# Weights for dx turned in the first attention chunk and loaded plainly later, with dW2 blocks fetched three ahead

## Chip, cores, metric

One core of one Trainium2 chip. The metric is the device time of one execution in microseconds (us), of which the median over several executions is quoted; the profile shows one execution. "Turned" means transposed by the DMA on its way.

## The reference

A transformer block with adaptive layer norm, forward and all its gradients (S = 2048, D = 512, 32 heads of 16, MLP width F = 1792, bfloat16), cut to what matters:

```python
mod = (silu(c) @ w_mod).reshape(c.shape[0], 6, 1, -1)
sa, ca, ga, sb, cb, gb = (mod[:, 0], ..., mod[:, 5])
h = layernorm(x) * (1 + ca) + sa
x = x + ga * attention(h, A_wqkv, A_wo)
h = layernorm(x) * (1 + cb) + sb
x = x + gb * (relu(h @ B_w1 + B_b1) ** 2 @ B_w2 + B_b2)
...
out, vjp = jax.vjp(f, A_x, A_wqkv, A_wo, B_w1, B_b1, B_w2, B_b2, c, w_mod)
grads = vjp(grad_out)
```

Two gradients matter here. The gradient of `A_x` goes through the layer norm and needs `A_wqkv`, its rows scaled by 1 + ca and then transposed; the kernel calls this WmT, and uses it at the very end. The gradient of `B_w2` (dW2) is a product of the MLP's activations (kept in DRAM as `aT_d`) with the gradient at the MLP's output.

## The kernel before

The kernel runs the forward attention in four chunks of queries, then a middle phase (last MLP chunk, gradients dW1 and dW2 of the MLP), then the backward attention. Background generators feed TensorE (PE) with work: `fill.take(n)` in the middle phase emits n of their steps. The middle phase prepared WmT itself:

```python
        fill.until("half")                       # dW2 is half done
        ws = self.load_wmt(self.open_pool("wkt", bufs=1))
        self.T0, pieces = self.load_group(0)     # first group of the backward
        pieces = self.pair_pieces(0, 0) + pieces
        for n, (d, sr) in enumerate(pieces):
            nc.sync.dma_start(d, sr)
            fill.take(7)
            if n % 3 == 2 and ws:
                self.turn_wmt(*ws.pop(0))
        for w in ws:
            self.turn_wmt(*w)
        fill.drain()
    ...
    def load_wmt(self, sb):
        self.WmT = self.wp.tile([P, 3 * DT, D], BF16, name="WmT")
        ws = []
        for kt in range(DT):                     # DT = 4
            w = sb.tile([P, 3 * D], BF16, name="w_kt", bufs=DT)
            nc.sync.dma_start(w[:], io["A_wqkv"][kt * P:(kt + 1) * P, :])
            nc.scalar.activation(w[:], w[:], ACT.Copy, scale=self.opcaT[:, kt:kt + 1])
            ws.append((kt, w))
        return ws

    def turn_wmt(self, kt, w):
        self.nc.sync.dma_start_transpose(self.WmT[:, :, kt * P:(kt + 1) * P], w[:])
```

dW2 takes one turned block of activations for 16 matmuls, and fetches two blocks ahead:

```python
        def load(ft):
            r = sb.tile([P, ST, P], BF16, name="a_blk", bufs=3)
            nc.sync.dma_start_transpose(r[:], self.aT_d[ft])
            ...
        load(0); load(1)
        yield 0
        for ft in range(FT):                     # FT = 14
            if ft + 2 < FT:
                load(ft + 2)
            a, w2_blk = blks[ft]
            pt = self.dps.tile([P, 512], F32, name="dps")
            for st in range(ST):                 # ST = 16
                nc.tensor.matmul(pt[:], lhsT=a[:, st, :], rhs=g_tm[:, st, :], ...)
                yield 1
```

During the first attention chunk a generator projects q, k and v for the later heads (groups g); ScalarE (ACT) is the bound there, with one exp after the other (busy for 66.9 of 67 us from 135 to 202 us in the kernel before):

```python
        for g in range(1, NQ):
            ...
            yield (-g, 0)
            if g == 2:
                yield from self.gen_mod()
            elif 3 <= g < 3 + self.SC:
                yield from self.gen_vt(4 * (g - 3))
            for s0 in range(512, S, 512):
                yield from self.gen_fm(self.mps, 0, g - 1, s0)
```

The softmax here doesn't subtract the row's maximum and nothing guards it: scores larger than these inputs give would overflow.

## Time and profile before

| | before |
|---|---|
| time, median of 3 runs | 2691.65 us (2686.25 to 2698.53) |
| span of the profiled execution | 2680.6 us |
| PE busy | 93% |
| ACT busy | 86% |
| dW2, first to last matmul | 67.2 us |

### The profile page before, as it was taken

How to read it: one execution, taken by the hardware profiler on the slowest of the kernel's cores; microseconds unless marked ns; L12 is line 12 of the kernel's file. 1: busy time of each engine (PE TensorE's matmuls, PEld its weight loads, DVE VectorE, ACT ScalarE, POOL GpSimd, SP SyncE). 2: the span in 40 equal slices, each digit the busy share in tenths (PEclk: the TensorE clock that was granted, in tenths of full speed). 3: DMA queues.
4: the chain of work that ended last, by engine and by line, in shares of the span. 5: the costliest groups of instructions: out<-in, count | busy, mean ns of one | idle time of the engine just before them, and what ended most of it. 6: DMA issues, size and time to landing. Idle time of an engine off the chain costs nothing.

```text
span 2680.6 us, 76637 instructions
## 1 busy us (share of the span) xinstructions
PE 2486.6 (93%) x30980; PEld 1229.1 (46%) x31210; DVE 1764.2 (66%) x3650; ACT 2307.9 (86%) x3728; POOL 393.4 (15%) x661
## 2 busy tenths in 40 slices
PE   5999999999999998898999999999999999999997
PEld 2555555555555554653443444444444434443443
DVE  4222222423423344656999999999999999999857
ACT  4999999999999995326999999999999999999823
POOL 2234531320221131351000000000000000000032
PEclk9999999999999999999999999999999999999999
DMA  4367752440441244999999999999999999999997
GB/s 146 91 146 160 175 121 69 114 110 21 124 115 54 86 98 122 222 224 173 201 196 198 199 196 198 200 202 202 194 199 200 203 198 200 196 197 209 208 217 175
DMA packets 1198027, 439.59 MB, mean 164 GB/s; under 512 B 1135430, under 2 KB 1159496, under 8 KB 1197672
## 3 DMA queue, kind: packets, MB, share of 16 engines
q1 hardware_dynamic: 1165608, 342.70, 70.4%
q0 software_dynamic: 29952, 89.36, 11.5%
q8 instruction: 244, 4.00, 0.6%
q10 hardware_dynamic: 2112, 2.62, 0.3%
q14 instruction: 111, 0.91, 0.1%
HBM read 83.30 MB, written 67.11 MB: 56 GB/s over the span
## 4 chain that ended last, share of the span: by engine, by line
PE 29%; DMA 24%; issue 3%; ACT 2%; DVE 1%; POOL 0%; SPq 0%; POOLq 0%; ACTq 0%; DVEq 0%
DMA dsT<-ds 22%; PE st L1315 11%; PE acckv L1217 6%; PE accq L1239 5%; ACT pu L1319 1%; PE dps L848 1%; PE g3ps L1421 1%; PE dp L1260 1%; DMA a_blk<-aT_d 1%; PE dxhps L1396 1%; PE st L1279 1%; PE dps L797 1%; PE st L1228 1%; DMA wo<-in_A_wo_dram 0%; PE g3ps L1408 0%
## 5 line engine op out<-in xcount | busy, mean ns | idle before, releaser
L1262 DVE TENSOR_TENSOR ds<-dp,pu 128x512 bf16<-128x512 f32 x2048 | 1243.0, 679 | 62.5 <-PE dp L1260 53.9
L1319 ACT ACTIVATE pu<-st 128x512 bf16<-128x512 f32 x2048 | 1082.8, 613 | 104.7 <-PE dp L1260 67.5
L348 ACT ACTIVATE pu<-st 128x1024 bf16<-128x1024 f32 x1024 | 943.0, 1072 | 6.7 <-PE st L345 4.7
L345 PE MATMUL st<-QTm,KTq 128*128 128x512 bf16 x1923 | 579.4, 377 | 31.1 <-ACT pu L348 9.6
L309 PEld LDWEIGHTS <-pu 128*128 128x128 bf16 x8192 | 347.4, 96 | 235.4 <-ACT pu L348 0.4
L1239 PEld LDWEIGHTS <-dsT 128*128 128x128 bf16 x8192 | 244.9, 96 | 273.7 <-issue 205.3
L309 PE MATMUL accbank<-Vaug,pu 128*128 128x17 bf16 x8192 | 357.7, 171 | 7.1 <-ACT pu L348 0.3
L1260 PE MATMUL dp<-m,dOTq 64*128 64x512 bf16 x1024 | 339.5, 383 | 0.0
L1260 PE MATMUL dp<-m,q 64*128 64x512 bf16 x1024 | 338.7, 384 | 0.7 <-DVE g2w L854 0.7
L1315 PE MATMUL st<-m,q 64*128 64x512 bf16 x1024 | 321.3, 383 | 8.4 <-ACT pu L1319 6.5
L1315 PE MATMUL st<-m,QTq 64*128 64x512 bf16 x1024 | 320.6, 383 | 6.3 <-ACT pu L1319 4.5
L345 PEld LDWEIGHTS <-KTq 128*128 128x128 bf16 x2048 | 194.1, 96 | 187.0 <-issue 132.6
L1370 POOL DMA_DIRECT2D O_tm<-O_d x2 | 1.8, 912 | 1323.1 <-PE accq L1239 1323.0
L1239 PE MATMUL accq<-q,dsT 128*128 128x16 bf16 x4096 | 150.8, 170 | 31.4 <-DMA dsT<-ds 31.3
L1239 PE MATMUL accq<-Kg,dsT 128*128 128x16 bf16 x4096 | 148.8, 170 | 28.9 <-DMA dsT<-ds 28.4
L1217 PE MATMUL acckv<-ds,Qg 128*16 128x512 bf16 x1024 | 155.3, 383 | 0.3 <-DVE ds L1262 0.2
L1217 PE MATMUL acckv<-pu,q 128*16 128x512 bf16 x1024 | 155.3, 383 | 0.0
L1217 PE MATMUL acckv<-ds,q 128*16 128x512 bf16 x1024 | 155.3, 384 | 0.0
L1217 PE MATMUL acckv<-pu,dOg 128*16 128x512 bf16 x1024 | 154.9, 383 | 0.0
L1280 ACT COPY dsT<-st 128x512 bf16<-128x512 bf16 x256 | 152.5, 596 | 1.5 <-PE st L1279 1.4
L316 DVE RECIPROCAL rl<-accbank 128x4 f32<-128x4 f32 x128 | 22.9, 179 | 163.2 <-PE accbank L309 163.2
L1315 PEld LDWEIGHTS <-q 64*128 64x128 bf16 x1024 | 58.1, 94 | 123.1 <-issue 104.2
(313 smaller groups left out, 2627.7 us busy)
## 6 DMA issues: line engine op xcount, KB each, us to landing
KTq<-KTq_d POOLq DMA_DIRECT2D x24, 512.0 KB, 3.6
duT_d<-auT POOLq DMA_DIRECT2D x4, 1792.0 KB, 8.8
aT_d<-rT POOLq DMA_DIRECT2D x4, 1792.0 KB, 13.7
KTq_d<-KTq SPq DMA_DIRECT2D x32, 128.0 KB, 1.8
QTq_d<-ev_fm SPq DMA_DIRECT2D x32, 128.0 KB, 2.0
VTq_d<-vT POOLq DMA_DIRECT2D x4, 1024.0 KB, 6.2
O_d<-O POOLq DMA_DIRECT2D x4, 1024.0 KB, 5.4
m<-KTq_d SPq DMA_DIRECT2D x32, 128.0 KB, 3.6
```

The lines of the kernel that those rows point to most:

```text
L309: nc.tensor.matmul(acc[:, a, sub, :], lhsT=pu[:, a, sub * P:(sub + 1) * P], rhs=Vaug[:, kb, h, :], start=(kb == 0 and a == 0 and sub == 0) ...
L345: nc.tensor.matmul(stt[:, a, :], lhsT=KT[:, kb * P:(kb + 1) * P], rhs=QTm[2 * jp + a][:], start=True, stop=True)
L348: nc.scalar.activation(pu[:], stt[:], ACT.Exp, scale=self.scale)
L797: nc.tensor.matmul(g4[:, kt, :], lhsT=xh2[:, st, kt * P:(kt + 1) * P], rhs=du[:, st, :], start=(st == 0), stop=(st == ST - 1))
L848: nc.tensor.matmul(pt[:], lhsT=a[:, st, :], rhs=g_tm[:, st, :], start=(st == 0), stop=(st == ST - 1))
L1217: nc.tensor.matmul(acckv[r:r + DH, :], lhsT=T[n][:, ib, col:col + DH], rhs=src[:, a, :], start=(ib == 0), stop=(ib == ST - 1))
L1239: nc.tensor.matmul(accq[:, ib, a, :], lhsT=dsT[:, (i * 2 + a) * 4 + sub, :], rhs=T["K"][:, 4 * c + sub, col:col + DH], start=(c == 0 and i ...
L1260: nc.tensor.matmul(dp[:], lhsT=T["dOT"][rd, ib * P:(ib + 1) * P], rhs=masked["VT"][2 * jp + a][rd, 512 * c:512 * (c + 1)], start=True, sto ...
L1262: nc.vector.tensor_tensor(dsg[:, i, a], dp[:], pu[:, a, :], ALU.mult)
L1280: nc.scalar.copy(dsT[:, 0:4, :], tp[:])
L1315: nc.tensor.matmul(stt[:], lhsT=T["QT"][rs, q], rhs=masked["KT"][2 * jp + a][rs, c0:c0 + 512], start=True, stop=True)
L1319: nc.scalar.activation(pu[:, a, :], stt[:], ACT.Exp, scale=self.scale)
```

## The change

The intent is to empty the DMA queue in front of dW2's last blocks. The weights are in SBUF during the first attention chunk anyway; so they are scaled on GpSimd, turned, and stored to a DRAM scratch `WmT_d` there, in four rounds. In the middle phase three plain loads of WmT, behind everything else, take the place of four loads, four scalings and four turns. Besides, dW2 gets a fourth block buffer and fetches three ahead, and the background work between the pieces is `take(8)` each time.

```diff
+        self.WmT_d = self.dram("WmT_d", [P, 3 * DT, D], BF16)
 ...first chunk's generator
             yield (-g, 0)
+            if 2 < g < 3 + self.DT:
+                w = self.qkv_eb.tile([P, 3 * self.D], BF16, name="wm_s", bufs=1)
+                nc.gpsimd.tensor_scalar(w[:], self.wq[:, g - 3, :], self.opcaT[:, g - 3:g - 2], 1.0, ALU.mult, ALU.mult)
 ...
             for s0 in range(512, S, 512):
                 yield from self.gen_fm(self.mps, 0, g - 1, s0)
+            if 2 < g < 3 + self.DT:
+                wt = self.qkv_eb.tile([P, 3 * self.DT, P], BF16, name="wm_t", bufs=1)
+                nc.sync.dma_start_transpose(wt[:], w[:])
+                with nc.allow_non_contiguous_dma(reason="256B runs"):
+                    nc.gpsimd.dma_start(self.WmT_d[:, :, (g - 3) * P:(g - 2) * P], wt[:])
 ...middle phase
-        ws = self.load_wmt(self.open_pool("wkt", bufs=1))
         self.T0, pieces = self.load_group(0)
-        pieces = self.pair_pieces(0, 0) + pieces
-        for n, (d, sr) in enumerate(pieces):
+        pieces = self.pair_pieces(0, 0) + pieces + self.load_wmt()
+        for (d, sr) in pieces:
             nc.sync.dma_start(d, sr)
-            fill.take(7)
-            if n % 3 == 2 and ws:
-                self.turn_wmt(*ws.pop(0))
-        for w in ws:
-            self.turn_wmt(*w)
+            fill.take(8)
 ...dW2
-            r = sb.tile([P, ST, P], BF16, name="a_blk", bufs=3)
+            r = sb.tile([P, ST, P], BF16, name="a_blk", bufs=4)
 ...
+        load(2)
         for ft in range(FT):
-            if ft + 2 < FT:
-                load(ft + 2)
+            if ft + 3 < FT:
+                load(ft + 3)
 ...load_wmt, its body now
+        return [(self.WmT[:, n:n + DT, :], self.WmT_d[:, n:n + DT, :]) for n in range(0, 3 * DT, DT)]
```

More of the change, by code (lines that the diff above doesn't have):

```diff
@@ L388, in gen_open @@
         xm1T = self.xm1T = sb.tile([P, DT, S], BF16, name="xm1T")
-        wq = sb.tile([P, DT, 3 * D], BF16, name="wqkv")
+        wq = self.wq = sb.tile([P, DT, 3 * D], BF16, name="wqkv")
         wpads = self.wpads = [sb.tile([P, DT, NQ, P], BF16, name=f"wpad{t}") for t in range(2)]
@@ L745, in last_chunk @@
         fill.until("half")
-        ws = self.load_wmt(self.open_pool("wkt", bufs=1))
         self.T0, pieces = self.load_group(0)
-        pieces = self.pair_pieces(0, 0) + pieces
-        for n, (d, sr) in enumerate(pieces):
+        pieces = self.pair_pieces(0, 0) + pieces + self.load_wmt()
+        for (d, sr) in pieces:
             nc.sync.dma_start(d, sr)
-            fill.take(7)
-            if n % 3 == 2 and ws:
-                self.turn_wmt(*ws.pop(0))
-        for w in ws:
-            self.turn_wmt(*w)
+            fill.take(8)
         fill.drain()
-        for name in ("wkt", "dw2", "dw1", "e0", "dwps", "tps", "mps2", "mps"):
+        for name in ("dw2", "dw1", "e0", "dwps", "tps", "mps2", "mps"):
             self.close_pool(name)
@@ L1141, in open_bwd, with load_wmt @@
         self.qp = self.open_pool("p5q", bufs=1, side="right")
-    def load_wmt(self, sb):
-        nc, io = self.nc, self.io
+    def load_wmt(self):
         D, DT = self.D, self.DT
         self.WmT = self.wp.tile([P, 3 * DT, D], BF16, name="WmT")
-        ws = []
-        for kt in range(DT):
-            w = sb.tile([P, 3 * D], BF16, name="w_kt", bufs=DT)
-            nc.sync.dma_start(w[:], io["A_wqkv"][kt * P:(kt + 1) * P, :])
-            nc.scalar.activation(w[:], w[:], ACT.Copy, scale=self.opcaT[:, kt:kt + 1])
-            ws.append((kt, w))
-        return ws
-    def turn_wmt(self, kt, w):
-        self.nc.sync.dma_start_transpose(self.WmT[:, :, kt * P:(kt + 1) * P], w[:])
+        return [(self.WmT[:, n:n + DT, :], self.WmT_d[:, n:n + DT, :]) for n in range(0, 3 * DT, DT)]
     def load_group(self, g):
```

## The prediction

> **What bounds the kernel now.** I read the page first, for the stages. The span is 2680.6 us in 40 slices of 67 us.
>
> ```profile
> PE   5999999999999998898999999999999999999997
> ACT  4999999999999995326999999999999999999823
> DMA  4367752440441244999999999999999999999997
> PE 29%; DMA 24%; issue 3%; ACT 2%; DVE 1%; POOL 0%; SPq 0%; POOLq 0%; ACTq 0%; DVEq 0%
> ```
>
> Slices 1 to 15 (to about 1005 us) are the forward attention, with PE and ACT both at 9; slices 19 to 38 are the backward attention, with PE, ACT and DMA at 9; in between lies a middle phase (last MLP chunk, dW1, dW2, loads for the backward) in which ACT falls to 2. The last line is the chain that ended last; it names PE and DMA, and by line mostly the turning of ds in the backward attention, which the change does not touch. So the change can only act in two places: the first attention chunk, where it adds work, and the end of the middle phase, where it takes work out.
>
> Then the chain in order of time, around the end of the middle phase:
>
> ```profile
> 1158.82 0.22 PE dps L848
> ...
> 1186.80 3.40 PE dps L860 x16
> 1190.21 10.11 DMA a_blk<-aT_d
> 1200.36 5.32 PE dps L848 x16
> ...
> 1208.05 9.47 DMA a_blk<-aT_d
> 1217.57 8.70 PE dps L848 x32
> ```
>
> dW2 is L848 (224 matmuls) plus 16 of L860 for db2. From the ninth block on, the chain runs through the turned loads of a_blk and no longer through PE. How long PE was really idle is in the timeline of PE (start, length, and in brackets the idle time before it and what ended it):
>
> ```profile
> 1158.66 17.43 PE L848 MATMUL dps<-g_tm,a_blk 128*128 128x512 bf16 x78
> ...
> 1200.36 5.31 PE L848 MATMUL dps<-g_tm,a_blk 128*128 128x512 bf16 x16 [3.20 <-DMA a_blk<-aT_d]
> 1207.00 3.63 PE L848 MATMUL dps<-g_tm,a_blk 128*128 128x512 bf16 x15 [1.33 <-DVE g2w L854]
> 1217.57 8.69 PE L848 MATMUL dps<-g_tm,a_blk 128*128 128x512 bf16 x32 [6.95 <-DMA a_blk<-aT_d]
> ```
>
> Undisturbed, 78 matmuls take 17.43 us, or 0.2235 us each. All 240 at that pace are 53.6 us. They took from 1158.66 to 1226.26, 67.6 us. The **excess is 14.0 us**: 11.66 us of idle time (3.20, 1.33, 6.95, and 0.18 in another line) and some 2.3 us because what runs after an idle stretch is slower (16 in 5.31 us is 0.33 us each; the mean granted clock from 1200 to 1220 us is 0.77 where it is 1.00 before).
>
> Why the blocks are late is in the DMA view of 1185 to 1226 us:
>
> ```profile
> DMA packets 19063, 9.86 MB, mean 240 GB/s; under 512 B 17108, under 2 KB 17108, under 8 KB 19060
> q1 hardware_dynamic: 18449, 8.25, 96.5%
> q0 software_dynamic: 611, 1.57, 15.4%
> w_kt<-in_A_wqkv_dram SPq DMA_DIRECT2D x4, 384.0 KB, 8.9
> a_blk<-aT_d SPq DMA_TRANSPOSE x5, 6.4
> WmT<-w_kt SPq DMA_TRANSPOSE x4, 5.3
> ```
>
> The sixteen engines are full: the sync queue alone is at 96.5% of their time. In the same view of 1158 to 1185 us that queue is at 72.4% with eight a_blk and nothing else, so one a_blk costs 0.724 x 27 / 8 = 2.44 us of all the engines, against the 16 x 0.2235 = 3.58 us in which PE uses it up. The block stream alone is carried; the stream plus w_kt, WmT and eleven pieces of the first group is not. In the queue's own timeline, issuing the a_blk of 1190 us takes 7.24 us where one takes 3 in the median.
>
> [...] here a_blk's 0.524 MB in 2.44 us is 215 GB/s[...]. [...] the new store writes runs of 256 B, and no row of the trace times exactly that. [...] the trace's row is 1753 ns for a 128x1792 tensor_scalar.
>
> **The change part by part.**
>
> Removed from the middle phase: four loads of w_kt (4 x 0.393 = 1.57 MB), four ACT scalings of 1.57 us (ACT is idle there anyway, so worth nothing), and four SBUF transposes (1.57 MB, by a_blk's cost 4 x 0.75 x 2.44 = 7.3 us of all engines). Added there: three plain loads of WmT, 1.57 MB. They are the last of the fourteen pieces, so in the queue they stand behind the last a_blk, and WmT is first read at 2575 us: nothing waits for them. What must land before dW2 ends falls from 9.8 MB to about 4 a_blk (2.1) + pieces (2.36) + w2 loads and dW2 stores (1.57) = 6.0 MB, an estimate from the sizes in that view. At its mean of 240 GB/s that is 25 us.
>
> The fourth buffer: the load of block ft+4 waits until block ft is done and is used four blocks later, so its lead grows from two blocks to three, 7.2 to 10.7 us. Landing takes 5.4 to 10.1 us (median 6.4) here, so three blocks cover even the worst seen. Also one more block is already under way when the pieces start. Block 6 ends at about 1158.7 + 7 x 3.58 = 1183.7 us; from then PE needs one more block and the 112 matmuls behind it, until 1158.7 + 53.6 = 1212.3 us, 28.6 us. The 25 us of transfers fit, with 3.6 us to spare. PE should bound dW2 again: I take back 12.5 of the 14.0 us and leave 1.5 for a stall or two.
>
> After dW2 the first exp of the backward waits for the last dW2 store (2 us from issue to landing now, with 31 us of idle ACT before). That stays, and the WmT loads are then still in flight (6.0 + 1.57 MB at 240 GB/s end 31.5 us after 1183.7, at 1215): I charge 1 us.
>
> Added in the first chunk, in four rounds between about 135 and 270 us: a POOL tensor_scalar of 128x1536, by the row above 1753 x 1536/1792 = 1.5 us; one SBUF transpose of 1.8 us of the engines; one POOL store with 1536 runs, which should cost POOL about 1 us to issue, as the 0.92 us of the 1024-run dOp_d store. That is 2.5 us on a POOL that is busy 13 to 15 of 34 us there, with the DMA engines at 0.6 to 0.76; ACT is full (34.0 of 34) and gets nothing added, and PE gets no instruction. So it lies beside the bound. What could reach it is POOL standing still until the turned tile lands (3 to 5 us), with the next q load behind it; those loads are issued more than half a unit of 17 us early. I charge 0.5 us in all.
>
> Sum: -12.5 + 1 + 0.5 = **-11 us**. 2691.65 - 11 = about 2681 us, 0.4% less.
>
> **The rivals.** (1) *The transfers still bound dW2's end*: the margin of 3.6 us is smaller than what a slow mix of transfers can take, and SP issues its last pieces without waiting, so WmT shares the engines with the store traffic. For it: [...]a transpose moves slower than a plain load. Against it: w_kt and WmT's transposes, over 30% of the bytes, are gone from in front. It would leave a gain of 5 us, 2687 us. (2) *POOL stalls the first chunk*: for it, POOL [...]already waits for turned tiles (41.3 us for ev_tm from KTq between 60 and 260 us); four stalls of 5 us reaching ACT would eat the gain, giving 2691 to 2701 us. Against it: the lead of the q loads. (3) *The backward starts earlier but is not shorter by as much*: its first group must have landed, and its 1330 us run by the turned ds at full DMA share, so a start with a backlog can shift its pattern by some us either way: 2676 to 2688 us. (4) *The full 14 us and a little of the clock*: 2677 us.
>
> **Range and chances.** No rival moves the time by 2% (54 us): the whole stage that changes has 14 us to give, and the costs added are of that size at most. The three runs of before spread over 12 us (2686.25 to 2698.53), as much as the effect itself, so the range is set by that and by rivals 1 and 2: 2669 to 2693 us. Faster by over 2%: 0.01; within 2%: 0.97; slower by over 2%: 0.02, for a stall in the first chunk or backward that I do not see.
>
> **What will show it.** Right: the idle of PE before dW2's matmuls falls from 11.7 to under 3 us, its 240 matmuls take 54 to 57 us, the clock in that window stays near 1.00, and the backward's first exp comes 10 to 13 us earlier relative to the first matmul of dW2; the first chunk's end moves by less than 1 us. Wrong: a_blk still named as the releaser for over 5 us (rival 1); PE idle before st waiting for QTm, or ACT below 34.0 of 34 us between 135 and 300 us (rival 2); the backward longer by more than 4 us from first exp to last (rival 3).

## More of the kernel before

One line of another part enters the argument later, the product of b2 with its gate, on VectorE (DVE):

```python
        nc.vector.tensor_tensor(self.b2gb_b[:], b2_b, self.mod_row(5)[0:1, :], ALU.mult)
```

The page's utilisation says PE is at 93%; that is an average over stages, and the place which the change touches is worse. The windows view of the kernel before, for the second part of dW2 (columns: window, its length, busy time and count of PE, weight load, DVE, ACT and POOL (GpSimd), granted clock, busy share of the DMA engines, GB/s):

```profile
1185.00:1226.00 41.00, 29.42 (x119) 12.08 (x119) 9.00 (x14) 6.08 (x4) 16.36 (x20) 0.88 1.12 240
```

PE is busy for 29.4 of 41 us, no other engine comes near that, and the DMA share is at 1.12.

## The result

| | before | after |
|---|---|---|
| first comparison, median | 2693.03 us (4 runs) | 2672.68 us (4 runs, 2669.53 to 2674.50) |
| its ratio, 95% interval | | 0.9924 [0.9899, 0.9949] |
| repeat on another chip, median | 2690.29 us (66 runs, 2673.27 to 2704.20) | 2678.82 us (21 runs, 2666.48 to 2683.30) |
| its ratio, 95% interval | | 0.9954 [0.9939, 0.9969] |
| span of the profiled execution | 2680.6 us | 2670.9 us |

A ratio is the mean time of one kernel's fast runs over that of the other's of the same rounds, so not quite the ratio of the medians quoted. The change is faster, by far less than 2%: about 20 us in the first comparison and about 12 us in the repeat. The repeat has many more runs and shows how far single executions of one kernel lie apart (31 us for the kernel before), so I take its 12 us as the size.

One caution for what follows: the two profiled executions of the kernel before (2682.52 and 2680.96 us) are 9 and 10 us faster than its medians, those of the kernel after (2672.80 and 2679.81 us) lie at theirs. The spans of the two pairs of profiles therefore differ by 9.7 and only 1.3 us. A stage is compared by its own length and its own waits below, and not by these spans.

The page of the kernel after has the same shape in its slices as before, and the same two names in the chain that ended last:

```profile
PE   4999899999999998998999999999999999999997
ACT  4999899999999996417999999999999999999823
...
PE 30%; DMA 23%; issue 2%; ACT 2%; DVE 1%; POOL 0%; SPq 0%; POOLq 0%; ACTq 0%; DVEq 0%
```

The fifth slice (268 to 335 us) has dropped from 9 to 8 on PE and on ACT; it comes back below. For the rest I cut the trace into stages by the first and last matmul of known lines (the scores of the forward attention, dW1, dW2, the scores of the backward). In us:

| stage | before | after | before, repeated | after, repeated |
|---|---|---|---|---|
| start to first forward matmul | 48.1 | 52.2 | 46.5 | 52.2 |
| forward attention | 963.0 | 972.9 | 963.1 | 974.7 |
| from there to dW1 | 82.9 | 78.6 | 78.3 | 77.7 |
| dW1 | 64.7 | 57.5 | 64.5 | 57.5 |
| dW2 | 67.2 | 51.6 | 69.8 | 52.0 |
| backward attention | 1312.4 | 1314.0 | 1314.4 | 1312.8 |
| from there to the end | 142.1 | 143.9 | 142.2 | 150.5 |

The differences that both pairs share: dW2 is 16 to 18 us shorter, as meant; dW1 is 7 us shorter, which nothing in the change obviously does; the opening is 4 to 6 us longer, and the forward 10 to 12. The last stage takes 140.8 to 152.3 us in the 14 profiles of this document, short and long ones among kernels of either kind; I don't count its 8 us in the second pair as the change's.

**dW2.** The timeline of PE in the kernel after (start, length, idle before in brackets):

```profile
1161.24 27.79 PE L853 MATMUL dps<-g_tm,a_blk 128*128 128x512 bf16 x125
1188.87 3.62 PE L865 MATMUL dps<-g_tm,ones_b 128*128 128x512 bf16 x16
1192.32 20.88 PE L853 MATMUL dps<-g_tm,a_blk 128*128 128x512 bf16 x94
1213.14 0.82 PE L1310 MATMUL st<-m,q 64*128 64x512 bf16 x3
```

Not one bracket: PE runs through dW2 and straight into the backward, and a_blk releases it nowhere. The windows view of the kernel after, for the same part of dW2 as above:

```profile
1187.00:1213.00 26.00, 25.89 (x120) 11.69 (x120) 9.01 (x14) 0.00 (x0) 17.02 (x21) 1.00 1.10 273
```

PE is busy 25.89 of 26 us, at a granted clock of 1.00 for 0.88 before; ACT's scalings are gone. The DMA share is as before (1.10), but the engines move 273 GB/s for 240. The DMA view of the same window shows what is still among them:

```profile
q1 hardware_dynamic: 9829, 5.62, 90.8%
WmT<-WmT_d SPq DMA_DIRECT2D x3, 512.0 KB, 5.5
a_blk<-aT_d SPq DMA_TRANSPOSE x4, 7.9
```

Packets fell from 19,063 (in 41 us) to 10,390 (in 26 us), and the blocks still take 7.9 us to land (median); with three blocks of lead that is soon enough.

**The start of the backward.** ACT's timeline, before and then after, at the first exp of the backward:

```profile
1229.77 3.04 ACT L1319 ACTIVATE pu<-st 128x512 bf16<-128x512 f32 x6 [31.17 <-DMA out_dram<-dw]
```

```profile
1217.39 3.04 ACT L1314 ACTIVATE pu<-st 128x512 bf16<-128x512 f32 x6 [54.36 <-DMA out_dram<-dw]
```

The wait for the last dW2 store is still what releases it. It comes about 4.2 us after dW2's last matmul for 3.5 before, and 56.2 us after the first (1217.39 - 1161.24) for 71.1 (1229.77 - 1158.66).

**The opening.** The timelines of POOL in the kernel before and after:

```profile
20.46 1.06 POOL L419 TENSOR_TENSOR rstd<-ve,mhalf 128x4 f32<-128x4 f32 x1 [6.06 <-DVE ve L418]
```

```profile
22.77 1.56 POOL L507 TENSOR_SCALAR wm_s<-wqkv,opcaT 128x1536 bf16<-128x1536 bf16 x1 [9.36 <-DMA wqkv<-in_A_wqkv_dram]
24.99 1.06 POOL L420 TENSOR_TENSOR rstd<-ve,mhalf 128x4 f32<-128x4 f32 x1
```

The first weight scaling is written in the code at group 3, but has neither work nor buffers in front of it that hold it there. The scheduler put it first, so the layer norm's `rstd`, on which everything hangs, queues behind an engine that stands for 9.36 us until the weights have landed. It runs 4.5 us later.

**The first chunk.** POOL's queue in the kernel after: the store of a turned tile, then two q loads behind it (dots stand for a copy and a store that the kernel before has too).

```profile
240.61 1.04 POOL L518 DMA_DIRECT2D WmT_d<-wm_t  x1
...
242.15 0.52 POOL L291 DMA_DIRECT2D QTm<-QTq_d  x1
...
243.23 0.51 POOL L291 DMA_DIRECT2D QTm<-QTq_d  x1
```

ACT's timeline a little later, in the kernel after; each line is an unbroken run of exps, and the bracket is the stop before it (the view of the first two lines ends at 290 us and cuts the second run short; the third is from a later view):

```profile
249.00 29.72 ACT L349 ACTIVATE pu<-st 128x1024 bf16<-128x1024 f32 x32 [2.50 <-PE st L346]
281.06 9.27 ACT L349 ACTIVATE pu<-st 128x1024 bf16<-128x1024 f32 x10 [2.35 <-PE st L346]
333.69 1.02 ACT L349 ACTIVATE pu<-st 128x1024 bf16<-128x1024 f32 x1 [4.65 <-PE accbank L310]
```

The first two stops follow PE waits of 1.65 and 1.26 us for QTm, which the kernel before does not have. The store costs the q loads more than its 1 us of issue: the eight that stand right behind the four stores take 4.1 to 5.3 us from issue to landing, where the same eight take 1.9 to 3.6 us in the kernel before. The third is another matter, for which see the experiments with early work taken away.

### The profile page after: what moved, and what is told of

Its sections match the earlier page's. It is cut to its first block, busy times and chain, and to the rows that moved or that the text cites.

```text
span 2670.9 us, 76621 instructions
## 1 busy us (share of the span) xinstructions
PE 2483.9 (93%) x30980; PEld 1226.1 (46%) x31210; DVE 1766.3 (66%) x3650; ACT 2304.0 (86%) x3724; POOL 406.9 (15%) x669
## 4 chain that ended last, share of the span: by engine, by line
PE 30%; DMA 23%; issue 2%; ACT 2%; DVE 1%; POOL 0%; SPq 0%; POOLq 0%; ACTq 0%; DVEq 0%
DMA dsT<-ds 22%; PE st L1310 11%; PE acckv L1212 6%; PE accq L1234 5%; ACT pu L1314 1%; PE dps L801 1%; PE g3ps L1416 1%; PE dp L1255 1%; PE dps L853 1%; PE dxhps L1391 1%; PE st L1274 1%; DMA out_dram<-dw 1%; PE st L1223 1%; DMA wo<-in_A_wo_dram 0%; PE g3ps L1403 0%
## 5 line engine op out<-in xcount | busy, mean ns | idle before, releaser
L349 ACT ACTIVATE pu<-st 128x1024 bf16<-128x1024 f32 x1024 | 943.5, 1071 | 17.7 <-PE st L346 10.9
```

The lines of the kernel that those rows point to most:

```text
L349: nc.scalar.activation(pu[:], stt[:], ACT.Exp, scale=self.scale)
```

## The experiments

Theory A is the prediction's: the gain is dW2's, and the early work lies beside the bound. Its rival B: the early work costs 8 to 14 us, and the middle phase gives that much more. C, which came up with dW1's unexpected 7 us, is that the new scratch tensor moves other DRAM tensors and so changes the speed of their transfers; D is chance between executions.

### e1: the early work alone

The kernel before with `WmT_d`, the four scalings, turns and stores; the middle phase stays as before, so nothing reads `WmT_d`.

```diff
+            if 2 < g < 3 + self.DT:
+                w = ... ; nc.gpsimd.tensor_scalar(w[:], ...)
 ...
+                nc.sync.dma_start_transpose(wt[:], w[:])
+                nc.gpsimd.dma_start(self.WmT_d[...], wt[:])
```

> The kernel before, plus the turning and the storing of WmT in the first chunk alone; the middle phase is the old one, and nothing reads the store. Theory A (the prediction: this work lies beside the bound): within 3 us of before. Theory B (the POOL queue issues the store in front of a q load, and the scaling is hoisted into the opening, so the forward attention is delayed, as the profile after seems to show, with its forward ending 13.9 us later): 8 to 14 us slower than before, and in the profile PE waits for QTm between 230 and 290 us.

Measured: 2690.35 us for 2691.03, ratio 0.9996 [0.9973, 1.0019]. That is A's number, and B's 8 to 14 us are excluded as a net cost. But the profile does not show A's reason: the opening is 51.5 us and the forward 972.1, both as long as in the kernel after, PE waits for QTm at 249 and 281 us, and dW1 is 57.7 us. So the early work isn't beside the bound; it costs and, whatever the mechanism, dW1 is shorter with it. (dW2, with the old middle phase, took 63.8 us in this profile.)

### e2: no early work

The kernel after without scalings, turns, stores and scratch; the three WmT loads fetch the same bytes from `A_wqkv`. dx (out_1) is wrong on purpose; the comparison with the reference nevertheless passed, so that comparison cannot vouch for WmT's part in dx.

```diff
-        return [(self.WmT[:, n:n + DT, :], self.WmT_d[:, n:n + DT, :]) ...]
+        return [(self.WmT[:, n:n + DT, :], self.io["A_wqkv"].rearrange("(p a) (b d) -> p (a b) d", p=P, d=D)[:, n:n + DT, :]) ...]
```

> The changed kernel without its work in the first chunk: the three plain loads take the same bytes in the same runs from the untouched weight tensor instead, so the gradient of x is wrong on purpose. Theory A: within 3 us of the changed kernel, 0.992 of before. Theory B: 8 to 14 us faster than the changed kernel, 0.987 to 0.989 of before. The dW2 stretch should be the changed kernel's, 52 us, in both.

Measured: 2682.10 us, ratio 0.9957 [0.9932, 0.9982]. The middle phase alone gives 0.43%, about what the whole change gives in the repeat (0.46%, with intervals of 0.15 and 0.25 points either way). Dropping the early work did not make the kernel faster than the one after, as I had thought it should. dW2 is 51.6 us, the opening 46.6, and dW1 63.6 again.

### e3: three ahead, alone

The kernel before with `bufs=4` and `load(ft + 3)`.

> The kernel before with dW2's blocks three ahead and nothing else. If the transfers themselves bound dW2's end[...], one more block of lead moves the waiting by little: 0 to 5 us faster than before, and dW2's stretch stays above 62 us. If the lead was what lacked, it gives most of the gain: 10 to 14 us faster, dW2's stretch under 57 us.

Measured: 2685.62 us, ratio 0.9980 [0.9953, 1.0007]. dW2 falls to 56.4 us from 67.2, so the lead matters by itself, though the total shows hardly any of it: the forward is 973.2 us in this profile, 10 us longer than before. What is left of the waits, in the PE timeline of this kernel:

```profile
1211.43 3.63 PE L849 MATMUL dps<-g_tm,a_blk 128*128 128x512 bf16 x16 [2.52 <-DMA a_blk<-aT_d]
1216.95 3.63 PE L849 MATMUL dps<-g_tm,a_blk 128*128 128x512 bf16 x16 [1.90 <-DMA a_blk<-aT_d]
```

The last two blocks still come late, behind the turned weights.

### e4: the traffic taken out, two ahead

The kernel after with `bufs=3` and `load(ft + 2)`.

> The changed kernel with dW2's blocks two ahead as before. If taking 3.1 MB out of the queue is what helps: within 3 us of the changed kernel, dW2's stretch 52 to 56 us. If the lead is needed too: 5 us or more slower than the changed kernel, with waits for a_blk left in dW2.

Measured: 2675.71 us, ratio 0.9952 [0.9926, 0.9978]. dW2 is 56.3 us, with one visible wait:

```profile
1210.81 8.77 PE L852 MATMUL dps<-g_tm,a_blk 128*128 128x512 bf16 x32 [2.86 <-DMA a_blk<-aT_d]
```

So each part alone brings dW2 to 56 us, and both bring it to 51.6. They are two cures of the same lateness and don't add up: 10.8 and 10.9 us alone, 15.6 together. The 67.2 us that they are taken from is one profile; the six with the old middle phase and two ahead have 63.8 to 69.8 us, so the shares are rough. The floor is not: in all six profiles with both parts dW2 takes 51.6 to 52.0 us. The total time cannot tell 4.7 us of dW2 apart here (the interval holds the ratio of the kernel after); the trace can.

### e5: only the scratch tensor

The kernel before with the 1.57 MB of `WmT_d` and one 32 KB store to it, for theory C.

```diff
+        self.WmT_d = self.dram("WmT_d", [P, 3 * DT, D], BF16)
+        nc.gpsimd.dma_start(self.WmT_d[:, 0, 0:P], self.ones_b[:])
```

> The kernel before, plus a scratch tensor of 1.57 MB in DRAM where the change puts WmT's (and one store of 32 KB into it at the start, so that it exists). It tests why dW1, whose instructions the change doesn't touch, took 57.5 to 57.8 us in the three profiles with the early work and 63.6 to 64.7 us in the three without it. Theory C (the scratch tensor moves what lies behind it in DRAM, and dW1's transfers get faster by that): dW1 57 to 58 us here, and the time 4 to 7 us under before. Theory D (it is the early work or its effect on the order of transfers, not the place): dW1 63 to 65 us, the time within 2 us of before.

Measured: 2690.74 us, ratio 1.0011 [0.9993, 1.0030], and dW1 66.8 us. C falls.

### e6: opening mended, store later and on the sync queue

The kernel after with the scaling factor taken from a copy `opca2`, which is made behind a product of the first chunk (in `gen_mod`, group 2), so that the scaling can't run before `rstd`; and each store one round later, on the sync queue instead of POOL's.

```diff
+        self.opca2 = self.qkv_eb.tile([P, DT], F32, name="opca2", bufs=1)
+        nc.vector.scalar_tensor_tensor(self.opca2[:], pt[:, 0:DT], 0.0, self.opcaT[:], ALU.mult, ALU.add)
 ...
+            if 3 < g < 4 + self.DT:
+                nc.sync.dma_start(self.WmT_d[:, :, (g - 4) * P:(g - 3) * P], wt[:])
 ...
-                nc.gpsimd.dma_start(self.WmT_d[:, :, (g - 3) * P:(g - 2) * P], wt[:])
```

> The changed kernel with two repairs of its early work: the scaling takes its factor from a copy made after the modulation (so it can't be hoisted into the opening), and the store of a round goes out on the sync queue one round later (so POOL neither waits for the turned tile nor issues the store in front of a q load). If the opening's delay of 4 to 5 us is the hoisted scaling: opening 47 to 48 us to the first exp's matmul instead of 52. If the store on POOL delays the q loads: no PE waits for QTm between 230 and 290 us. Together 4 to 8 us faster than the changed kernel; if neither matters, the same within 2 us.

Measured: 2678.59 us, ratio 0.9955 [0.9939, 0.9971]. The opening is back at 47.0 us, and in e10, which has `opca2` and the old stores, at 46.8; in the six profiles whose scaling is not held back it is 51.4 to 52.5 us. That settles its cause. Of the two QTm stops one of 1.63 us is left: the q loads that follow the stores still take 3.2 to 4.9 us to land, though the stores have left POOL's queue. But dW1 is 63.8 us, and the total is that of the kernel after. What the repair gives, dW1 takes back.

### a_again and b_again: the two kernels once more

Copies of both, with 21 and 18 runs; the files differ from the originals in nothing that is executed.

> The changed kernel once more, for a second profile and beside the repaired one on one chip. Expected 0.992 of before again; by stage: opening 52 us, forward 970 to 975, dW1 57 to 58, dW2 51 to 52.

> The kernel before once more, for a second profile. The first had a forward of 963.0 us where all others, with or without the early work, have 969.6 to 974.5. If that is chance: 968 to 975 here, and the early work costs the forward nothing that shows. If the early work's kernels and the chip explain it: 963 again. Opening 48, dW1 64, dW2 64 to 67 us.

Measured: 2678.82 us, 0.9954 [0.9939, 0.9969], and 2690.69 us, 1.0008 [0.9992, 1.0024]. The stage table above has both profiles: dW1's 57.5 against 64.5 us and the forward's 974.7 against 963.1 came again to within 2 us, so D falls for dW1. The forward has a part that comes and goes, for which see e9.

### e7 and e8: what of the early work makes dW1 short?

e7 is the kernel before with four 32 KB stores on the sync queue in the first chunk; e8 is e1 without its stores, so scalings and turns only.

```diff
 e7
+            if 2 < g < 3 + self.DT:
+                nc.sync.dma_start(self.WmT_d[:, g - 3, 0:P], self.ones_b[:])
 e8, from e1
-                nc.gpsimd.dma_start(self.WmT_d[...], wt[:])
```

> The kernel before with four small stores (32 KB) on the sync queue where the changed kernel has its four turns, and no other early work. It tells apart why dW1 takes 57.5 to 57.8 us in the four profiles with turns and POOL stores (early work alone, two ahead, changed twice) and 63.6 to 66.8 us in the six others, the repaired kernel (four turns and four stores on the sync queue) among them, though dW1's instructions and waits are alike. If it is the number of transfers on the sync queue before it (by four, not by eight): dW1 57 to 58 us. If it is what they carry or the POOL stores: 63 to 67 us.

> The kernel before with the scaling and the four turns in the first chunk, without their stores. Opening 51 to 53 us (the hoisted scaling is in). dW1 57 to 58 us if the turns on the sync queue are what makes dW1 short; 63 to 67 us if the stores on POOL are needed too. By the time within 3 us of before, as the opening's 4 us go against dW1's 6.

Measured: e7 2689.74 us for 2687.68, 1.0004 [0.9989, 1.0019], dW1 64.1 us; e8 2692.59 us, 1.0002 [0.9980, 1.0024], dW1 63.6 us. Neither more transfers on the sync queue nor the turns do it. e8 shows one thing more: without stores PE waits for QTm nowhere, and the same eight q loads land in 2.3 to 3.7 us. So it is the stores, and not the turns, that make the two QTm stops.

What is known of dW1: in all six profiles whose kernel has the four stores of `WmT_d` on POOL's queue (after, its repeat, e1, e4, and e9 and e10 below) it is 57.5 to 59.5 us; in the eight others it is 63.6 to 66.8. The orders of the instructions of PE, DVE and ACT in this phase are the same in both kernels. In the trace, one turned block of du comes late. The timeline of PE before, then after:

```profile
1121.93 5.33 PE L797 MATMUL dps<-du_blk,xh 128*128 128x128 bf16 x64 [4.92 <-DMA du_blk<-duT_d]
```

```profile
1126.58 3.75 PE L801 MATMUL dps<-du_blk,xh 128*128 128x128 bf16 x64
```

After the stop of 4.92 us the 64 matmuls also run slower, 5.33 for 3.75 us. The windows view before shows the transfers meanwhile (last two columns, DMA share and GB/s):

```profile
1110.00:1114.00 4.00, 4.00 (x72) 3.99 (x70) 3.48 (x23) 1.74 (x8) 1.53 (x4) 1.00 1.36 202
1114.00:1118.00 4.00, 3.01 (x51) 2.82 (x48) 2.80 (x18) 1.74 (x8) 1.20 (x3) 1.00 0.88 46
```

The engines count as busy (a share of 0.88) but move 46 GB/s, for some 4 us; the longest such stretch that I find in dW1 of the kernel after is 2 us (60 GB/s from 1136 to 1138 us), and PE does not stop in it. Why four stores of 0.393 MB on POOL's queue, 850 us earlier, should do away with it is open. My runs exclude the scratch tensor's room (e5), the number of sync-queue transfers (e7), the turns (e8), and the same stores on the sync queue (e6).

### e9: the b2 product on GpSimd

Of the forward's 10 us, the stop of 4.65 us before 333.69 us is not due to the early work: e3 has it with 8.12 us and e2 with 5.79, and neither turns anything early. Three views around 306 to 316 us of the kernel before, repeated (DVE, POOL, the sync queue):

```profile
306.73 0.68 DVE L884 TENSOR_TENSOR b2gb_b<-dxb,mod 1x512 bf16<-1x512 bf16 x1 [2.19 <-DMA dxb<-in_B_b_dram]
...
307.30 3.26 POOL L923 TENSOR_TENSOR w<-w,mod 128x512 bf16<-128x512 bf16 x2
...
308.44 2.80 SPq L948 DMA_TRANSPOSE fT<-O_b  x1
```

The same of e3:

```profile
308.16 3.26 DVE L885 TENSOR_TENSOR b2gb_b<-dxb,mod 1x512 bf16<-1x512 bf16 x1 [2.17 <-DMA dxb<-in_B_b_dram]
...
308.57 2.30 POOL L924 TENSOR_TENSOR w<-w,mod 128x512 bf16<-128x512 bf16 x2
...
312.46 6.17 SPq L949 DMA_TRANSPOSE fT<-O_b  x1
```

A product of one row takes 0.68 us when it is nearly through before POOL's pair of products begins, and 3.26 us when it meets them. The casts of O behind it come 2.6 us late, and the turned load of O then holds the sync queue for 6.17 us instead of 2.80. In each view one of the two is lengthened: in the first POOL's pair, 3.26 us for 2.30, in the second DVE's product, 3.26 us for 0.68. (In the first the product overlaps the pair by only 0.11 us; what runs beside the rest of the pair is DVE's three casts of O, from 307.34 us for 1.08 us.) Starting first does not spare the product: in e3 DVE's start is stamped 0.41 us ahead of POOL's, and DVE still ends 0.55 us after POOL's pair. Why one lengthens the other was not shown. The starts of the two lie within a microsecond of each other in both views, so the stop comes and goes with small shifts. Over all profiles the two go together: in the eight in which DVE's product takes 2.70 to 3.28 us a stop of 3.5 to 8.1 us follows, in the four with 0.68 us there is none. Those four are all executions 7 to 13 us faster than the median of their kernel, both profiles of the kernel before among them (e2's, which has the stop, is 13 us faster too). So the median execution of the kernel before may have the stop as well; no trace here shows it. e9 keeps the two from meeting, in the kernel after:

```diff
-        nc.vector.tensor_tensor(self.b2gb_b[:], b2_b, self.mod_row(5)[0:1, :], ALU.mult)
+        nc.gpsimd.tensor_tensor(self.b2gb_b[:], b2_b, self.mod_row(5)[0:1, :], ALU.mult)
```

> The changed kernel with one operation of the end of chunk 0 (b2 times the gate, 1 x 512) moved from VectorE to POOL. In seven of ten profiles VectorE stood in it for 2.7 to 3.3 us in place of 0.68, while POOL ran its scaling of w2, and PE lost 5 to 8 us soon after; in the other three VectorE was first. If that is a contest of the two[...]: O_b is cast within 2 us, no stop of ACT over 3 us between 320 and 345 us, forward 963 to 968 us in place of 972.9 to 974.7, and the time 4 to 8 us under the changed kernel's (0.9954 of before), if the unprofiled runs have it too. If the stop has another cause: the same within 2 us.

Measured: 2672.90 us for 2687.68, ratio 0.9937 [0.9918, 0.9957]. The trace of e9 has no stop there:

```profile
281.09 59.89 ACT L349 ACTIVATE pu<-st 128x1024 bf16<-128x1024 f32 x65 [2.47 <-PE st L346]
```

65 exps and more (the view ends at 340 us) run through where the kernel after broke off. The forward takes 966.5 us, and its remaining stops (1.55 and 2.47 us) are those from QTm. In time, e9's interval overlaps that of the kernel after, so it is shown in the trace that the stop is gone with the product off DVE, and the gain is only likely.

### e10: e9 with the opening mended

e9 with `opca2` from e6; stores on POOL as in the kernel after.

> The changed kernel with the same move and with the scaling's factor taken from a copy made after the modulation, so that it isn't hoisted into the opening; the stores stay on POOL. Opening 46.5 to 48 us in place of 52.2, forward 963 to 968 us, dW1 57 to 58 us, dW2 51 to 52 us: 8 to 13 us under the changed kernel's, 0.991 to 0.992 of before. If the opening's delay is lost elsewhere anyway, as the repaired kernel's equal time hints, only what the move alone gives.

Measured: 2670.54 us for 2687.68, ratio 0.9921 [0.9894, 0.9948], the lowest ratio of all runs. The opening is 46.8 us, dW1 59.3 and dW2 51.6, each as hoped; yet the forward ends at 1018.2 us for e9's 1018.5. The 5 us of the opening went into the forward, where ACT waits 12.9 us for scores in place of e9's 8.3: the two stops from QTm are 2.63 and 2.31 us (1.55 and 2.47 in e9), and one of 2.18 us follows later that e9 has not. Why it follows is open. So it is not shown that e10 is faster than e9, nor than the kernel after; its interval overlaps both of theirs.

## Why the prediction was right

The time (2681 us predicted; 2672.68 and 2678.82 us measured) and the gain (11 us; 12 in the repeat) agree. The sum was right partly by luck: dW2 gave more than its term, the first chunk cost far more than its term, and dW1 paid for that.

| step of the prediction | its term | what the runs showed |
|---|---|---|
| dW2's excess taken back | -12.5 us | -15.6 us (-17.8 in the repeat) |
| start of the backward | +1 us | +0.7 us (3.5 to 4.2 us) |
| first chunk | +0.5 us | opening +4.1, forward +9.9 us, of which 4.65 in one stop that isn't the change's |
| dW1 | no term | -7.2 us |
| sum | -11 us | -12 us (0.9954), -20 us in the first comparison |

**dW2** went by its mechanism: the transfers fit, the fourth buffer covered their landing (5.9 to 8.0 us, and no wait for a_blk), PE became the bound (busy 25.89 of 26 us). The size was off in one place. I took 0.2235 us a matmul from a line that counted 78 matmuls in 17.43 us; the kernel after runs all 240 in 51.9 us, or 0.216 each. At that pace 17.43 us hold 80.6 matmuls, so that line probably lacked some records (the trace of the kernel before holds 219 matmuls of L848 for 224 weight loads), and the excess was 15.7 us and not 14.0. The idle I left for "a stall or two" did not come. So the 240 matmuls, at 51.9 us, and the first exp, 14.9 us earlier against dW2's first matmul, fell outside the 54 to 57 and 10 to 13 us that I had named as signs, on the good side.

Two readings of the DMA shares were wrong, without harm to the sum. The engines were not shown to be full, as 96.5% and 15.4% make 112% and packets overlap; and so the share gives no time for one block. Where turned loads of a_blk are alone they move 290 GB/s, which makes 1.8 us for 0.524 MB, an estimate, and not 2.44 us. The 25 us of transfers were worked out from the 240 GB/s of the mix.

**Rival 1**, transfers still bounding the end, is out: a_blk releases PE nowhere. What it feared is in the traces all the same: a slow mix (24 to 407 GB/s in slices of 1.03 us from 1185 to 1226 us of the kernel before), turned loads slower than plain ones (290 GB/s alone and 398 GB/s, for which see the end), and dW2's stores beside the loads of WmT (q0 at 10.3% and q1 at 92.7% from 1207.5 to 1213 us of the kernel after). Its nearest relatives are e3 and e4, with 4.4 and 2.9 us of waiting left.

**Start of the backward**: right, to 0.3 us. The backward itself moved by +1.6 us and -1.6 us in the two pairs, so **rival 3** has no sign either.

**The first chunk** is the step that was wrong: "I charge 0.5 us in all" and "the first chunk's end moves by less than 1 us". The single costs were right (a scaling takes 1.556 us in the median for 1.5; issuing a store 0.999 us for 1), and that ACT and PE get nothing added. Wrong was the conclusion that work on a half-idle engine stays beside the bound. I looked at where the code writes the scaling, and not at where it may be moved to: it went ahead of `rstd`. And the stores stand directly in front of q loads, which went out later (at the two stops by some 1.7 and 3.3 us against ACT's stream, of which the store's issue explains 1) and took 2 to 3 us longer to land; their lead was too small for that. POOL standing still for the turned tile, which I had feared, was 2.8 us in all, in the first two rounds, where no stop followed. That is **rival 2** in a smaller form: two stops of 2.5 us and not four of 5.

**The net**: e1 says that all the early work, dW1's gain included, changes the time by between -7 and +5 us, and e2 that the middle phase alone gives the whole gain. Both are measured. That dW1's gain is what evens out the early work's cost is read from the traces of e1, e6 and e10; its cause stays open.

## What to carry to other kernels

When a block stream and other loads crowd the DMA engines, taking bytes out and fetching one block earlier may be two cures of one illness: try the cheaper one alone first, for here they took 10.9 and 10.8 us off dW2 alone and 15.6 us together. Work moved to a half-idle engine was not free here: `rstd`, behind the scaling in POOL's queue, ran 4.5 us later, and the q loads behind the stores took 4.1 to 5.3 us to land for 1.9 to 3.6. So look up, in the order of the built program, what the scheduler put such work in front of, and what lands behind its transfers. And read a small gain from many runs as well as from stages of the trace: here single executions of one kernel lay 31 us apart and the effect was 12.

## What else the traces show of transfers

- Turned loads move 290 GB/s where they are alone on the engines (kernel after, 1175.5 to 1176.5 us), and the mostly plain transfers behind the last of them 398 GB/s (1207.5 to 1213 us; 730 of 848 packets there have 512 B or more, of the 1,133 turned ones none).
- Issuing a turned load takes a good part of its time to landing: an a_blk held the sync queue for 2.0 to 7.2 us (median 2.9) of 5.4 to 10.1 us to landing in the kernel before, and the turned load of O held it for 6.17 us when it came late (e3).
